# Storing the token tiles in reverse order and streaming them from last to first

## The chip, the cores and the metric

The kernel runs on one core of a Trainium2 chip. The metric is the device time of one execution in microseconds, the median of several runs. Before the change that is 657.98 us (three runs, 657.59 to 659.76).

## The reference

The inputs are q, k and v of shape (8, 8, 576, 64) in float32, two weight matrices of a first feed-forward layer (512 x 2048 and 2048 x 512), and those of a "soft" mixture of experts. Cut to what matters here:

```
x   = attention(q, k, v)                 # 4608 tokens x 512, linear attention
h   = x @ moe_w_in                       # 4608 x 2048
x2  = (h * cos(h)) @ moe_w_out           # 4608 x 512
out = soft_moe(x2, phi, w1, w2)          # logits over 32 slots, softmax both ways
```

Tokens are rows. No result depends on the order in which a product visits its tokens, as long as each result lands in the place of its token.

## The kernel before, in words

The 4608 tokens are taken in nine blocks of 512. For each block b the attention leaves x transposed in PSUM, 128 features on the partitions and tokens along the free axis. It is then split into two tiles in SBUF: XH holds x rounded to the type fp32r in which the product is formed, XL the rest x - XH. ScalarE makes XH (`x_hi`, lines 592 to 598), VectorE makes XL from PSUM and XH (`x_lo`, lines 600 to 608). In blocks 0 and 1 one instruction covers one group of 128 features and all 512 tokens (lines 598 and 608); from block 2 on one instruction covers 128 tokens of all four feature groups, through `x_views` (lines 595 and 603). That is 36 instructions on either engine, all of 128x512 elements.

Two pairs of tiles alternate, as the index `b % 2` in lines 573 to 578 says: blocks 0, 2, 4 and 6 use the pair XH0/XL0, blocks 1, 3, 5 and 7 the pair XH1/XL1. Block 8 is cut into two halves of 256 tokens, each in one tile named xe that holds both parts.

The first layer's product is `mm1` (lines 911 to 927). A block has 16 steps, one for each 128 columns of moe_w_in, and a step has 12 matmuls: four groups of features, and for each of them three products, (W high, XH), (W high, XL) and (W low, XH). The weights W are the stationary operand, a fresh 128x128 load ahead of each matmul; the token tile is streamed, 512 columns (256 in block 8):

```
for n, (wi, xi) in enumerate(((0, 0), (0, 1), (1, 0))):
    nc.tensor.matmul(
        out=u_t[s], lhsT=w[:, wi, kk, o:o + 128], rhs=x[xi][:, kk],
```

That makes 8 x 16 x 12 = 1536 matmuls of 512 columns and 2 x 16 x 12 = 384 of 256 columns, all at line 925. Each step's product lies in one of three PSUM buffers (ps_h). ScalarE or VectorE rounds it (line 933 or 935), VectorE takes the fraction (941), ScalarE the sine (946), VectorE multiplies (949), TensorE adds the step to the logits (963) and VectorE transposes the result in blocks of 32 (970).

The order of all instructions on every engine is fixed by a table of numbers, PLACES, by which the operations are sorted when the program is built. The change does not touch it: every engine issues the same instructions in the same order before and after. `mm1` of a block's first step waits for the four `x_lo` of its block; three ring buffers of ps_h tie the product to the work of the other engines three steps back.

Of the kernel before, what the change touches and what calls it, by code (L numbers as in the profile page):

```python
# [10 lines left out]
F32 = mybir.dt.float32  # L11
# [5 lines left out]
ALU = mybir.AluOpType  # L17
# [262 lines left out]
def attention_cosine_moe_softmoe(  # L280
# [21 lines left out]
    nc = tc.nc  # L302
# [16 lines left out]
    def pst(tag, bufs):  # L319
        return ps.tile([128, 512], F32, tag=tag, name="ps_" + tag, bufs=bufs)  # L320
# [140 lines left out]
    pm_t = {}  # L461
# [107 lines left out]
    def x_parts(b, t):  # L569

        i = b % 2
        if b < NB - 1:
            if xh[i] is None:
                xh[i] = sbt([128, 4, 512], "XH1", F32R)
                xl[i] = sbt([128, 4, 512], "XL1", F32R)
            return [(xh[i][:, t], xl[i][:, t], slice(0, 512))]
        if not xe:
            xe.extend(sbt([128, 2, 4, 256], tag, F32R, name="xe") for tag in ("XH0", "XL0"))
        return [(e[:, 0, t], e[:, 1, t], slice(256 * n, 256 * n + 256)) for n, e in enumerate(xe)]

    def x_views(b, e):


        x_parts(b, 0)
        px = pm_t["x", e].rearrange("p (t n) -> p t n", t=4)
        if b < NB - 1:
            o = slice(128 * e, 128 * e + 128)
            return px, xh[b % 2][:, :, o], xl[b % 2][:, :, o]
        o = slice(128 * (e % 2), 128 * (e % 2) + 128)
        return px, xe[e // 2][:, 0, :, o], xe[e // 2][:, 1, :, o]  # L590

    def x_hi(b, t):
        if b > 1:
            px, hi, lo = x_views(b, t)
            nc.scalar.copy(out=hi, in_=px)
            return
        for hi, lo, o in x_parts(b, t):
            nc.scalar.copy(out=hi, in_=pm_t["x", t][:, o])

    def x_lo(b, t):  # L600
        if b > 1:
            px, hi, lo = x_views(b, t)
            nc.vector.tensor_tensor(out=lo, in0=px, in1=hi.bitcast(F32), op=ALU.subtract)
            pm_t.pop(("x", t))
            return
        px = pm_t.pop(("x", t))
        for hi, lo, o in x_parts(b, t):
            nc.vector.tensor_tensor(out=lo, in0=px[:, o], in1=hi.bitcast(F32), op=ALU.subtract)

    def k_max(b, tp, part):  # L610

# [277 lines left out]
    u_t, t_t, lt_t = {}, {}, {}  # L889
# [4 lines left out]
    def tile_of(d, i):  # L894

        return (i + (12 if 0 < d < 8 and d % 2 == 0 else 8 if d == 8 else 0)) % NF
# [14 lines left out]
    def mm1(s, ks):  # L911
        d, f = divmod(s, NF)
        b, t0, nt = parts[d]
        f = tile_of(d, f)
        if ks[0] == 0:
            u_t[s] = pst("h", 3)[:, 0:nt]
        w = w_t[f // 2]
        o = 128 * (f % 2)
        x = (
            (xh[b % 2], xl[b % 2]) if nt == 512  # L920
            else [xe[t0 // 256][:, i] for i in range(2)]
        )
        for kk in ks:
            for n, (wi, xi) in enumerate(((0, 0), (0, 1), (1, 0))):
                nc.tensor.matmul(  # L925
                    out=u_t[s], lhsT=w[:, wi, kk, o:o + 128], rhs=x[xi][:, kk],
                    start=(kk == 0 and n == 0), stop=(kk == 3 and n == 2),
                )

# [582 lines left out]
    def q_ops(b):  # L1512
# [18 lines left out]
        if b > 1:  # L1531
            for t in range(4):
                op(("q_mul", b, t), None, 0, q_mul, b, t, after=[("q_rec", b)],
                   ways=[(POOL, 1.0, True, ()), (DVE, 0.6, True, ())])
                op(("q_blk", b, t), DVE, 0.63, q_blk, t, after=[("q_mul", b, t)])
            for bb in range(max(b - 1, 1), min(b, 7) + 1):
                if ("kv_in", bb) not in isu.ops:
                    op(("kv_in", bb), DMA, 2.0, kv_in, bb, more=1.9, data=True,
                       after=[("kv_out", bb), ("q_kv", max(bb - 1, 1), 1)])
            op(("q_kv", b, 1), PE, 1.95, q_kv4, b, take="m", n_take=4,  # L1540
               after=[*each("q_blk", b), past("kv_in", b), past("kv_in", b - 1),
                      past("mm1", 16 * b - 17)])
            for t in range(4):
                op(("x_hi", b, t), ACT, 0.48 if b < 8 else 0.6, x_hi, b, t,
                   after=[("q_kv", b, 1)])
                op(("x_lo", b, t), DVE, 0.6 if b < 8 else 0.67, x_lo, b, t,
                   give="m", after=[("x_hi", b, t)])
            return
        for tp in range(2):
            for t in (2 * tp, 2 * tp + 1):  # L1550
                op(("q_mul", b, t), None, 0, q_mul, b, t,
                   ways=[(POOL, 1.0, True, ()), (DVE, 0.6, True, ())],
                   after=[("q_rec", b)] + [past("q_tr", b if tp else b - 1, 1 - tp, h) for h in (0, 1)])
            for h in range(2):
                op(("q_tr", b, tp, h), PE, 0.48, q_tr, tp, h, take="m",
                   after=[("q_mul", b, 2 * tp), ("q_mul", b, 2 * tp + 1), past("q_kv", b - 1, tp)])
                op(("q_tr_ev", b, tp, h), None, 0, q_tr_ev, tp, h, give="m",
                   ways=[(ACT, 0.48, False, ()), (DVE, 0.6, False, ())],
                   after=[("q_tr", b, tp, h), past("q_kv", b if tp else b - 1, 1 - tp)]
                   + ([past("k_bc", b), past("k_bc", b + 1)] if b < 2 else []))  # L1560
            op(("q_kv", b, tp), PE, cost, q_kv, b, tp, take="m", n_take=2,
               after=[("q_tr_ev", b, tp, 0), ("q_tr_ev", b, tp, 1), past("k_fin", b),
                      past("k_fin", b - 1), past("mm1", 16 * b - 17)] + raw_x)
            for t in (2 * tp, 2 * tp + 1):
                op(("x_hi", b, t), ACT, 0.48 if b < 8 else 0.6, x_hi, b, t,
                   after=[("q_kv", b, tp)])
                op(("x_lo", b, t), DVE, 0.6 if b < 8 else 0.67, x_lo, b, t,
                   give="m", after=[("x_hi", b, t)])
# [43 lines left out]
    def step_ops(s):  # L1612
# [13 lines left out]
        for ks in ((0,), (1,), (2,), (3,)) if s == 0 else (range(4),):  # L1626
            op(("mm1", s) if ks[-1] == 3 else ("mm1", s, ks[-1]), PE,
               (0.7 if nt == 512 else 0.355) * len(ks),
               mm1, s, ks, take=None if ks[0] else "h",
               after=[("x_lo", b, kk) for kk in ks] * (f == 0) + [past("cD", w)] * (b == 0)  # L1630
               + [("mm1", s, ks[0] - 1) if ks[0] else past("mm1", s - 1)]
               + [past("g", s - 3)] * (ks[0] == 0))
# [246 lines left out]
```

## Time and profile before

| what | value |
|---|---|
| median of three runs | 657.98 us (657.59 to 659.76) |
| the profiled execution | 659.31 us |
| its span, first to last instruction | 657.4 us |
| TensorE busy | 625.2 us, 95% of the span |
| VectorE busy | 534.9 us, 81% |
| ScalarE busy | 365.6 us, 56% |
| GpSimd busy | 128.2 us, 20% |
| granted TensorE clock, mean | 0.986 of full speed |
| share of the last-ending chain on TensorE | 80%, of it line 925 54% |

The profiled execution is 1.33 us longer than the median; 1.9 us of its time lie outside its span. In the profile PE is TensorE's matmuls, PEld its weight loads, DVE is VectorE, ACT ScalarE, POOL GpSimd. A matmul's row shows its start and a modelled duration that runs over the start of the next one, so that the pace of a stream of matmuls is read from the distance of their starts.

### The profile page before, as it was taken

What the parts mean: (1) busy time and instruction counts of PE and PEld (TensorE: products, weight loads), DVE (VectorE), ACT (ScalarE), POOL (GpSimd) and SP (SyncE); (2) the same over time, 40 slices, a digit from 0 to 9 for tenths busy, and PEclk for the clock granted to TensorE, in tenths of its full rate; (3) what the DMA queues carried; (4) which work ended last, traced back from release to release, by engine and by line L of the source; (5) the groups of instructions that cost most, each with busy time, mean ns of one, the idle gap of its engine ahead of it and who ended that gap; (6) DMA issues with size and microseconds to landing.
All of it is one profiled execution on the core that took longest, in us unless ns stands there. A gap on an engine that the chain in (4) does not pass through costs nothing.

```text
span 657.4 us, 18204 instructions
## 1 busy us (share of the span) xinstructions
PE 625.2 (95%) x7745; PEld 472.3 (72%) x7745; DVE 534.9 (81%) x1075; ACT 365.6 (56%) x642; POOL 128.2 (20%) x131
## 2 busy tenths in 40 slices
PE   5999999999999999999999999999999999999990
PEld 4677777687868777877788788778878889853540
DVE  7889999989998988979979887878988888852251
ACT  4899988576465376446456452443645465530051
POOL 4435546052132043040230101001110000000000
PEclk9799999999999999999999999999999999999996
DMA  9998955264312242143212400013001518899968
GB/s 320 304 408 291 351 163 148 98 154 128 91 49 76 80 114 82 49 113 99 67 31 67 138 0 2 1 37 94 1 1 48 211 35 332 328 386 412 421 242 347
DMA packets 60992, 103.88 MB, mean 158 GB/s; under 512 B 9456, under 2 KB 40560, under 8 KB 55920
## 3 DMA queue, kind: packets, MB, share of 16 engines
q1 hardware_dynamic: 60912, 102.74, 45.9%
q8 instruction: 60, 0.98, 0.6%
q14 instruction: 20, 0.16, 0.1%
HBM read 88.15 MB, written 14.57 MB: 156 GB/s over the span
## 4 chain that ended last, share of the span: by engine, by line
PE 80%; DMA 7%; DVE 6%; ACT 2%; issue 1%; POOL 1%; SPq 0%; DVEq 0%; ACTq 0%
PE ps_h L925 54%; PE ps_m L1110 6%; PE ps_LT L963 4%; PE ps_m L713 2%; PE ps_m L528 2%; PE ps_m L1357 2%; DMA rwo<-in_moe_w_out_dram 2%; DMA Q<-in_q_dram 2%; PE ps_LT L1699 2%; DMA KVB<-in_k_dram 1%; DMA out_dram<-ob 1%; DMA G<-in_moe_w_out_dram 1%; PE ps_h L1315 1%; PE ps_m L1315 1%; DVE qm L422 1%
## 5 line engine op out<-in xcount | busy, mean ns | idle before, releaser
L925 PE MATMUL ps_h<-XH,W 128*128 128x512 f32 x1024 | 330.1, 397 | 2.2 <-DVE G L949 2.2
L925 PEld LDWEIGHTS ps_h<-XH,W 128*128 128x128 f32 x1024 | 192.3, 188 | 56.8 <-issue 7.1
L925 PE MATMUL ps_h<-XL,W 128*128 128x512 f32 x512 | 201.0, 393 | 0.0
L946 ACT ACTIVATE T<-T 128x512 f32<-128x512 f32 (+1 forms) x160 | 92.7, 587 | 90.8 <-DVE T L941 90.4
L933 ACT ACTIVATE T<-ps_h,quarter 128x512 int32<-128x512 f32 (+1 forms) x123 | 79.3, 646 | 87.0 <-PE ps_h L925 86.6
L949 DVE TENSOR_TENSOR G<-T,ps_h 128x512 f32<-128x512 f32 (+1 forms) x160 | 99.2, 623 | 21.0 <-ACT T L946 15.7
L925 PEld LDWEIGHTS ps_h<-XL,W 128*128 128x128 f32 x512 | 96.2, 188 | 20.0
L941 DVE SCALAR_TENSOR_TENSOR T<-T,ps_h 128x512 f32<-128x512 int32 (+1 forms) x160 | 98.9, 622 | 10.6 <-ACT T L933 9.4
L970 DVE STREAM_TRANSPOSE G<-G 128x512 f32<-128x512 f32 (+1 forms) x160 | 98.2, 637 | 0.3 <-PE ps_LT L963 0.2
L425 POOL TENSOR_TENSOR Q<-Q,qm 128x512 f32<-128x512 f32 x33 | 34.8, 1072 | 153.7 <-DVE qm L422 128.2
L689 POOL TENSOR_TENSOR KVB<-KVB,km 128x576 f32<-128x576 f32 x22 | 33.3, 1539 | 72.3 <-DVE km L682 51.3
L925 PE MATMUL ps_h<-xe,W 128*128 128x256 f32 x384 | 46.7, 281 | 0.0
L925 PEld LDWEIGHTS ps_h<-xe,W 128*128 128x128 f32 x384 | 45.3, 189 | 1.6 <-DVE G L949 0.8
L446 POOL TENSOR_TENSOR Q<-Q,qm 128x512 f32<-128x512 f32 x27 | 27.9, 1061 | 82.6 <-DVE qm L439 63.3
L963 PE MATMUL ps_LT<-G,wphi 128*32 128x128 f32 (+1 forms) x1280 | 38.7, 264 | 0.8 <-issue 0.8
L963 PEld LDWEIGHTS ps_LT<-G,wphi 128*32 128x32 f32 x1280 | 30.4, 109 | 8.9 <-issue 6.7
L1110 PE MATMUL ps_m<-G,A 32*32 32x512 f32 x1024 | 35.7, 597 | 0.0
L946 ACT ACT_TABLE_LOAD x24 | 30.8, 1283 | 0.4
L935 DVE TENSOR_SCALAR T<-ps_h 128x512 int32<-128x512 f32 (+1 forms) x37 | 22.7, 614 | 7.1 <-PE ps_h L925 6.9
L422 DVE TENSOR_REDUCE qm<-Q 128x8 f32<-128x512 f32 x36 | 24.0, 672 | 3.2 <-DMA Q<-in_q_dram 3.2
L1110 PEld LDWEIGHTS ps_m<-G,A 32*32 32x32 f32 x1024 | 16.9, 103 | 13.4 <-issue 8.1
L1128 DVE SCALAR_TENSOR_TENSOR gacc<-gacc,ac,ps_m 128x512 f32<-128x512 f32 x32 | 23.2, 732 | 2.3 <-PE ps_m L1110 2.3
(214 smaller groups left out, 715.6 us busy)
## 6 DMA issues: line engine op xcount, KB each, us to landing
w_u<-in_moe_w_dram SPq DMA_DIRECT2D x22, 1024.0 KB, 8.1
KVB<-in_k_dram SPq DMA_DIRECT2D x16, 576.0 KB, 5.1
KVB<-in_v_dram SPq DMA_DIRECT2D x32, 256.0 KB, 4.4
out_dram<-ob SPq DMA_DIRECT2D x8, 1024.0 KB, 8.9
rwi<-in_moe_w_in_dram SPq DMA_DIRECT2D x7, 1024.0 KB, 9.9
G<-in_moe_w_dram SPq DMA_DIRECT2D x7, 1024.0 KB, 7.0
rwo<-in_moe_w_out_dram SPq DMA_DIRECT2D x5, 1024.0 KB, 10.5
wo<-G SPq DMA_DIRECT2D x16, 256.0 KB, 4.5
```

The lines of the kernel that those rows point to most:

```text
L422: nc.vector.reduce_max(out=qm[:, t], in_=qv(t), axis=AX.X)
L425: (nc.vector if eng == "DVE" else nc.gpsimd).tensor_tensor(out=qv(t), in0=qv(t), in1=qm[:, t].unsqueeze(2).to_broadcast([128, 8, 64]), op= ...
L446: (nc.vector if eng == "DVE" else nc.gpsimd).tensor_tensor(out=qv(t), in0=qv(t), in1=qs[:, t].unsqueeze(2).to_broadcast([128, 8, 64]), op= ...
L689: (nc.vector if eng == "DVE" else nc.gpsimd).tensor_tensor(out=k_t[:, t], in0=k_t[:, t], in1=km[:, t].unsqueeze(1).to_broadcast([128, KC, ...
L925: nc.tensor.matmul(out=u_t[s], lhsT=w[:, wi, kk, o:o + 128], rhs=x[xi][:, kk], start=(kk == 0 and n == 0), stop=(kk == 3 and n == 2),)
L933: nc.scalar.activation(out=t.bitcast(I32), in_=u_t[s], func=ACTF.Identity, bias=quarter)
L941: nc.vector.scalar_tensor_tensor(out=t, in0=t.bitcast(I32), scalar=0.25, in1=u_t[s], op0=ALU.subtract, op1=ALU.subtract)
L946: nc.scalar.activation(out=t_t[s], in_=t_t[s], func=ACTF.Sin, scale=-UNDER_TWO_PI)
L949: nc.vector.tensor_tensor(out=g_of(s), in0=t_t.pop(s), in1=u_t.pop(s), op=ALU.mult)
L963: nc.tensor.matmul(out=lt_t[d][32 * c:32 * c + 32, 0:w], lhsT=w2sb[:, f], rhs=g[:, w * c:w * c + w], start=(f0 == 0), stop=(f0 == NF - 1),)
L970: nc.vector.transpose(out=g_of(s), in_=g_of(s))
L1110: nc.tensor.matmul(out=st["gp"][i][32 * c:32 * c + 32].rearrange("p (f b) -> p f b", f=NF) if d < NB else st["gp"][i][32 * c:32 * c + 32]. ...
```

## The change

The tokens of a block are stored in XH and XL in reverse order: token n of the block in column 511 - n (in block 8, column 255 - n of its half). For this the copies read PSUM backwards, and from block 2 on write their 128 tokens into the mirrored slice of columns. The products then stream the columns backwards, with a step of -1, so that the results in PSUM stand in the natural order again.

```diff
--- before.py
+++ after.py
@@ -582,11 +582,11 @@
         x_parts(b, 0)
-        px = pm_t["x", e].rearrange("p (t n) -> p t n", t=4)
+        px = pm_t["x", e].rearrange("p (t n) -> p t n", t=4)[:, :, ::-1]
         if b < NB - 1:
-            o = slice(128 * e, 128 * e + 128)
+            o = slice(384 - 128 * e, 512 - 128 * e)
             return px, xh[b % 2][:, :, o], xl[b % 2][:, :, o]
-        o = slice(128 * (e % 2), 128 * (e % 2) + 128)
+        o = slice(128 - 128 * (e % 2), 256 - 128 * (e % 2))
         return px, xe[e // 2][:, 0, :, o], xe[e // 2][:, 1, :, o]
@@ -595,7 +595,7 @@
         for hi, lo, o in x_parts(b, t):
-            nc.scalar.copy(out=hi, in_=pm_t["x", t][:, o])
+            nc.scalar.copy(out=hi, in_=pm_t["x", t][:, o][:, ::-1])
@@ -605,7 +605,7 @@
         for hi, lo, o in x_parts(b, t):
-            nc.vector.tensor_tensor(out=lo, in0=px[:, o], in1=hi.bitcast(F32), op=ALU.subtract)
+            nc.vector.tensor_tensor(out=lo, in0=px[:, o][:, ::-1], in1=hi.bitcast(F32), op=ALU.subtract)
@@ -923,7 +923,7 @@
                 nc.tensor.matmul(
-                    out=u_t[s], lhsT=w[:, wi, kk, o:o + 128], rhs=x[xi][:, kk],
+                    out=u_t[s], lhsT=w[:, wi, kk, o:o + 128], rhs=x[xi][:, kk, ::-1],
                     start=(kk == 0 and n == 0), stop=(kk == 3 and n == 2),
                 )
```

## Rows read from the trace of the kernel before

**Rows 1.** The page: busy time and share, then the granted clock in 40 slices.
```profile
PE 625.2 (95%) x7745; PEld 472.3 (72%) x7745; DVE 534.9 (81%) x1075; ACT 365.6 (56%) x642; POOL 128.2 (20%) x131
...
PEclk9799999999999999999999999999999999999996
```

**Rows 2.** The page: the chain that ended last, by engine and by line.
```profile
PE 80%; DMA 7%; DVE 6%; ACT 2%; issue 1%; POOL 1%; SPq 0%; DVEq 0%; ACTq 0%
PE ps_h L925 54%; PE ps_m L1110 6%; PE ps_LT L963 4%; PE ps_m L713 2%; PE ps_m L528 2%; PE ps_m L1357 2%; DMA rwo<-in_moe_w_out_dram 2%; DMA Q<-in_q_dram 2%; PE ps_LT L1699 2%; DMA KVB<-in_k_dram 1%; DMA out_dram<-ob 1%; DMA G<-in_moe_w_out_dram 1%; PE ps_h L1315 1%; PE ps_m L1315 1%; DVE qm L422 1%
```

**Rows 3.** Groups by line and shape, TensorE: busy us, mean ns, idle before.
```profile
L925 PE MATMUL ps_h<-XH,W 128*128 128x512 f32 x1024 | 330.1, 397 | 2.2 <-DVE G L949 2.2
L925 PE MATMUL ps_h<-XL,W 128*128 128x512 f32 x512 | 201.0, 393 | 0.0
L925 PE MATMUL ps_h<-xe,W 128*128 128x256 f32 x384 | 46.7, 281 | 0.0
```

**Rows 4.** Timeline of TensorE in block 4 (pair XH0/XL0): start us, us.
```profile
328.70 0.39 PE L925 MATMUL ps_h<-XL,W 128*128 128x512 f32 x1
328.93 0.63 PE L925 MATMUL ps_h<-XH,W 128*128 128x512 f32 x2
329.40 0.40 PE L925 MATMUL ps_h<-XL,W 128*128 128x512 f32 x1
...
344.80 0.40 PE L925 MATMUL ps_h<-XL,W 128*128 128x512 f32 x1
```

**Rows 5.** The same in block 3 (pair XH1/XL1).
```profile
267.09 0.39 PE L925 MATMUL ps_h<-XL,W 128*128 128x512 f32 x1
...
282.73 0.39 PE L925 MATMUL ps_h<-XL,W 128*128 128x512 f32 x1
```

**Rows 6.** The same in block 8 (xe tiles).
```profile
539.66 12.99 PE L925 MATMUL ps_h<-xe,W 128*128 128x256 f32 x108
```

**Rows 7.** Timeline of the weight loads in block 4.
```profile
328.47 0.19 PEld L925 LDWEIGHTS ps_h<-XL,W 128*128 128x128 f32 x1
328.71 0.42 PEld L925 LDWEIGHTS ps_h<-XH,W 128*128 128x128 f32 x2
329.17 0.19 PEld L925 LDWEIGHTS ps_h<-XL,W 128*128 128x128 f32 x1
```

**Rows 8.** Busy time by stretch: us, PE, PEld, DVE, ACT, POOL, PEclk, DMA, GB/s.
```profile
104.00:164.00 60.00, 60.00 (x846) 46.94 (x845) 55.92 (x115) 40.20 (x66) 22.12 (x19) 1.00 0.44 124
...
328.24:345.04 16.80, 16.80 (x74) 13.54 (x72) 12.04 (x22) 9.74 (x15) 5.76 (x4) 1.00 0.16 36
266.64:282.96 16.32, 16.32 (x74) 13.51 (x72) 15.21 (x31) 7.24 (x12) 4.45 (x4) 1.00 0.18 50
```

**Rows 9.** Groups by line and shape, VectorE and ScalarE: the copies into XH and XL.
```profile
L603 DVE TENSOR_TENSOR XL<-ps_m,XH 128x512 fp32r<-128x512 f32 x24 | 15.9, 675 | 0.2
L608 DVE TENSOR_TENSOR XL<-ps_m,XH 128x512 fp32r<-128x512 f32 x8 | 5.5, 694 | 1.1 <-ACT XH L598 1.0
...
L595 ACT CAST XH<-ps_m 128x512 fp32r<-128x512 f32 x24 | 13.2, 587 | 6.2 <-PE ps_m L528 6.2
L598 ACT CAST XH<-ps_m 128x512 fp32r<-128x512 f32 x8 | 4.6, 594 | 1.1 <-PE ps_m L565 1.1
```

**Rows 10.** The same view: two VectorE reads of PSUM, line 1294 every fourth element.
```profile
L1294 DVE TENSOR_SCALAR KVB_u<-ps_m,esacc 128x512 f32<-128x512 f32 x1 | 0.8, 751 | 2.6 <-PE ps_m L1285 2.6
L1329 DVE TENSOR_SCALAR hs<-ps_h,mask 128x512 f32<-128x512 f32 x1 | 0.8, 751 | 8.5 <-PE ps_h L1315 8.5
```

**Rows 11.** The chain that ended last, in order of time: start us, us.
```profile
28.27 0.59 ACT XH L598
...
238.11 1.88 DVE XL L603 x3
```

## The prediction

> **What bounds the kernel now.** I read the page first, then the chain that ended last, then the groups by line, and last the timeline of single matmuls. The page shows TensorE busy for 95% of the span, with the clock at its full level in all but the first and the last slices [rows 1]. The chain says that this is no accident of averaging: 80% of it is TensorE, and 54% of the span is line 925, the streamed product of the first layer [rows 2]. The groups show that these matmuls almost never wait: 2.2 us of idle time in front of 1024 of them and none in front of the other 896 [rows 3]. So from about 30 to 575 us the end is set by the pace at which line 925 streams columns, and that is the operand that the change turns round.
>
> The durations in the groups overlap, so the pace has to be read from starts. In block 4 the (W high, XL) matmul, one in three, starts at 328.70 and 23 periods later at 344.80: 16.10 us for 69 matmuls, 233.3 ns each [rows 4]. In block 3 it is 15.64 us for 69, 226.7 ns each [rows 5]. In block 8 the last of 108 half-length matmuls starts 12.99 - 0.28 = 12.71 us after the first [rows 3, 6]: 118.8 ns for 256 columns. All three lie above the pure column time at the granted 2.4 GHz, 213.3 and 106.7 ns (the granted share was 1.00 in the first two stretches [rows 8]): by 20.0 ns, by 13.3 ns, and by 12.1 ns.
>
> This excess is the interesting part. Blocks 3 and 4 use the same weights, the same PSUM buffers and the same instructions; what differs is the pair of token tiles. The engine waits for nothing in either. So something small is lost while the columns are read, and how much depends on where the read tile lies. Each weight load starts with a matmul, takes 0.19 us and so runs beside the streaming [rows 7]: it is the nearest candidate for what the stream meets, but the trace doesn't prove it.
>
> **The change, part by part.**
>
> *The ScalarE copies (x_hi), 36 of them.* They read PSUM backwards instead of forwards and write as many elements: 587 and 594 ns each, some 20 us in all with the four of block 8, which are of the same shape [rows 9]. ScalarE is busy for 56% of the span [rows 1].
>
> *The VectorE subtractions (x_lo), 36 of them.* 675 and 694 ns each, some 24 us in all [rows 9]. Does reading PSUM in another order cost VectorE anything? The nearest row is line 1294, which reads PSUM at every fourth element and takes 751 ns; line 1329, the same operation read in order, takes 751 ns too [rows 10]. I take 0 for both engines. The upper bound is a doubling. Most of it would lie under TensorE's stream, because a block's copies run while the steps of the block before are still being streamed; on the chain these copies appear for only 0.59 us and 1.88 us [rows 11], so a doubling puts some 2.5 us on the path. If that cover went, VectorE would be late first: it was busy for 55.92 of 60 us in the stretch from 104 to 164 [rows 8]. Below nothing I see no way: the row that reads out of order is no faster either.
>
> *The mirrored slices.* From block 2 on, each copy writes the mirrored 128 columns. A matmul reads all four slices and waits for all four copies, before and after, so it makes no difference which slice comes first: 0.
>
> *The matmuls, 1536 of 512 columns and 384 of 256.* Same number, same order, same weight loads; the moving operand has a step of -1. No row of this trace has such an operand. The bounds: below, the whole excess goes, 768 x 20.0 + 768 x 13.3 + 384 x 12.1 ns = 15.4 + 10.2 + 4.6 = 30.2 us less (each pair of tiles has four of the eight full blocks). Above, a backward read could run at one column in the time of two: 1536 x 213.3 + 384 x 106.7 ns = 369 us more. Between ends so far apart I take the value nearest to the rows that are nearest: every column is still read once, neighbours still follow neighbours, and both pairs of tiles stay where they are, so the pace of each pair stays, 0.
>
> The Trainium skill, page "TensorE: Matmul & The Clock Gate", section "Step-by-step: what each phase is for", says that TensorE reads the moving operand and the weights through two ports of their own, so that the next weights take no read bandwidth from the running matmul. By that rule nothing between the two reads could depend on a direction and the sum would be 0; by the rows, with two paces for two pairs of tiles, it may be anything from -30 to a similar gain in the other direction. The same skill, page "SBUF — State Buffer", section "Specifications (TRN2)", gives SBUF 16-byte lines of which at least two hits are needed for full bandwidth; a step of -1 has four hits per line like a step of 1, so this page speaks against a halved rate. No run here shows either.
>
> **The sum.** 0 + 0 + 0. The sum is made on the profiled execution (span 657.4 us, 659.31 us in all), which is 1.33 us above the median of the runs; as the sum is a difference of 0, I forecast the median, 658.0 us. A measurement of this kernel can tell about 0.3% from no change, 2.0 us. In the pace that is little: 1536 + 384/2 = 1728 matmuls of full length, so 1.15 ns of 230 decide.
>
> **The rivals.**
>
> *Fewer meetings in the stream (faster).* If the excess comes from two reads that meet, turning one of them round changes how often. For it: the excess exists, it depends on the tile, and it is not waited for. Against it: nothing says which direction is the better one. Prices: if the blocks of XH0/XL0 only reached the pace of XH1/XL1, 768 x 6.7 ns = 5.1 us less, 653; if the whole excess went, 30.2 us less, 628. VectorE would give some of that back, as it has only 4 us free in 60 in the early blocks [rows 8]. I put the middle at half the excess, 15 us: 643 us.
>
> *More meetings in the stream (slower).* The same mechanism with the other sign, in the same place: each matmul of line 925 takes longer, TensorE stays the bound and everything behind it moves. From a mean pace of (233.3 + 226.7) / 2 + 1.15 = 231.2 ns on it decides. Prices: all at the pace of XH0/XL0, 768 x 6.7 ns = 5.1 us more, 663; the excess doubled, 30.2 us more, 688. Nothing on the other engines would hide it, since line 925 is on the chain with its whole length [rows 2].
>
> *A backward read at half the rate (slower).* Each matmul takes its column time once more: 658 + 369 = 1027 us. Three matmuls would then take over 1.3 us in place of 0.70. For it only that no row shows the form; it is a cliff, so there is no middle.
>
> That the change doesn't do what it says would show as forward reads and unchanged rows; the instructions of every engine are the same in number and order, so it can't be told from the first case by time.
>
> **How the numbers follow.** Unchanged pace 0.35 (656 to 660 us by itself), fewer meetings 0.30, more meetings 0.22, half the rate 0.13. The likeliest is the unchanged pace, 658.0 us. Within 0.3%: 0.33, leaving 0.02 of the first case for copies that come a little late. Faster: 0.30. Slower: 0.02 + 0.22 + 0.13 = 0.37. The half rate is left out of the range, and the outer ends of the two neighbours with it, 0.07 together: from 634 us, 24 of the 30 us of excess gone, to 688 us, the excess doubled.
>
> **What would show it.** Right: in blocks 3 and 4 three matmuls of line 925 take 0.680 and 0.700 us as before, the idle time in front of them stays at about 2 us, and lines 595, 598, 603 and 608 keep their mean durations within 20 ns. Fewer or more meetings: that period moves, in both pairs or in one, while weight loads keep their 0.19 us. Half rate: the modelled duration of a full matmul jumps by some 200 ns. The copies are wrong if lines 595 or 603 take over 1 us and line 925's idle time grows. The whole argument is wrong if the period stays and the end moves, because then the pace of line 925 wasn't what set it.

## The result and the profile after

| | before | after |
|---|---|---|
| median of nine runs on the same chips | 659.76 us (657.59 to 663.08) | 665.34 us (662.72 to 667.79) |
| ratio after / before | | 1.0081, 95% interval 1.0055 to 1.0107 |
| the profiled execution, its span | 659.31 us, 657.4 us | 662.72 us, 660.8 us |

The kernel became slower by 0.8%: 0.0081 x 659.76 = 5.3 us, by the interval 3.6 to 7.1 us. The page of the changed kernel, busy times, granted clock and the two lines of the chain:

```profile
PE 628.6 (95%) x7745; PEld 471.6 (71%) x7745; DVE 534.7 (81%) x1075; ACT 366.0 (55%) x642; POOL 128.3 (19%) x131
...
PEclk8999999999999999999999999999999999999996
...
PE 77%; DMA 8%; DVE 5%; ACT 4%; SPq 2%; issue 1%; DVEq 0%; ACTq 0%
PE ps_h L925 55%; PE ps_m L1110 6%; PE ps_LT L963 4%; DMA w_u<-in_moe_w_dram 3%; PE ps_m L528 2%; PE ps_m L713 2%; DMA KVB<-in_k_dram 2%; DMA out_dram<-ob 1%; PE ps_h L1315 1%; DMA rwi<-in_moe_w_in_dram 1%; SPq L388 1%; PE ps_LT L1699 1%; DMA A<-kd 1%; DVE G L970 1%; PE ps_m L1033 1%
```

The same engine at the same clock, the same number of instructions, and line 925 still has more than half of the chain (55%, 54% in [rows 2]). TensorE alone is busy longer, by 3.4 us; VectorE, ScalarE and GpSimd stand within 0.5 us of [rows 1]. The groups by line and shape of the changed kernel say where (busy us, mean ns, idle before):

```profile
L925 PE MATMUL ps_h<-XH,W 128*128 128x512 f32 x1024 | 333.8, 401 | 3.1 <-DVE G L949 3.1
L925 PE MATMUL ps_h<-XL,W 128*128 128x512 f32 x512 | 203.4, 397 | 0.0
...
L925 PEld LDWEIGHTS ps_h<-XL,W 128*128 128x128 f32 x512 | 96.3, 188 | 21.4 <-DVE XL L608 0.2
L925 PE MATMUL ps_h<-xe,W 128*128 128x256 f32 x384 | 47.2, 283 | 0.0
...
L603 DVE TENSOR_TENSOR XL<-ps_m,XH 128x512 fp32r<-128x512 f32 x24 | 15.9, 674 | 0.2
L595 ACT CAST XH<-ps_m 128x512 fp32r<-128x512 f32 x24 | 13.2, 586 | 6.3 <-PE ps_m L528 6.3
...
L608 DVE TENSOR_TENSOR XL<-ps_m,XH 128x512 fp32r<-128x512 f32 x8 | 5.4, 686 | 0.4 <-ACT XH L598 0.4
L598 ACT CAST XH<-ps_m 128x512 fp32r<-128x512 f32 x8 | 4.7, 601 | 1.1 <-PE ps_m L565 1.1
```

The three groups of line 925 are busy for 3.7, 2.4 and 0.5 us more than in [rows 3] (they overlap, so these are not to be added), and the idle time in front of them grew by only 0.9 us. The copies stand within 8 ns of [rows 9]: here reading PSUM backwards cost neither engine anything. The weight loads keep the 188 ns that they had before:

```profile
L925 PEld LDWEIGHTS ps_h<-XL,W 128*128 128x128 f32 x512 | 96.2, 188 | 20.0
```

So it is the pace, and the timeline of TensorE shows which pace. Block 3, the pair XH1/XL1, the same 69 matmuls as in [rows 5] (start us, us):

```profile
267.04 0.40 PE L925 MATMUL ps_h<-XL,W 128*128 128x512 f32 x1
...
283.14 0.40 PE L925 MATMUL ps_h<-XL,W 128*128 128x512 f32 x1
...
328.43 0.40 PE L925 MATMUL ps_h<-XL,W 128*128 128x512 f32 x1
...
344.53 0.40 PE L925 MATMUL ps_h<-XL,W 128*128 128x512 f32 x1
```

The second pair of lines is block 4, the pair XH0/XL0, as in [rows 4]. Both stretches now take 16.10 us, 233.3 ns a matmul. Block 4 took that before too; block 3 took 15.64 us, 226.7 ns. The difference between the two pairs of tiles is gone, and it went on the slow side.

Over whole blocks, as the mean distance of neighbouring starts inside the steps (the few wider than 290 ns left out), blocks 0, 2, 4 and 6 have 233.3 ns in both kernels, and blocks 1, 3, 5 and 7 go from 227.9 to 233.4 ns. That is 768 x 5.5 ns = 4.2 us. Block 8 takes 59.33 us from the start of its first to that of its last matmul in place of 58.76, 0.6 us more. The sum, 4.8 us, lies inside the measured 3.6 to 7.1.

The two profiled executions lie 3.4 us apart. The stretch from the first to the last start of a full matmul shows the same thing in them (the kernel before, then the changed one; us, PE busy, and so on as in [rows 8]):

```profile
31.24:516.46 485.22, 478.90 (x5688) 374.08 (x5685) 430.64 (x820) 295.73 (x492) 115.76 (x110) 1.00 0.34 105
30.13:518.41 488.28, 482.82 (x5689) 374.21 (x5685) 430.32 (x820) 296.44 (x492) 114.88 (x110) 1.00 0.34 105
```

TensorE is busy for 3.9 us more in it; 0.9 us of that is taken back by shorter waits.

### The profile page after: what moved, and what is told of

Read it like the earlier page. It is cut to its first block, busy times and chain, and to the rows that moved or that the text cites. A ratio compares the mean times of both kernels' runs of the same rounds, so it can differ in the third digit from the quotient of the medians.

```text
span 660.8 us, 18204 instructions
## 1 busy us (share of the span) xinstructions
PE 628.6 (95%) x7745; PEld 471.6 (71%) x7745; DVE 534.7 (81%) x1075; ACT 366.0 (55%) x642; POOL 128.3 (19%) x131
## 4 chain that ended last, share of the span: by engine, by line
PE 77%; DMA 8%; DVE 5%; ACT 4%; SPq 2%; issue 1%; DVEq 0%; ACTq 0%
PE ps_h L925 55%; PE ps_m L1110 6%; PE ps_LT L963 4%; DMA w_u<-in_moe_w_dram 3%; PE ps_m L528 2%; PE ps_m L713 2%; DMA KVB<-in_k_dram 2%; DMA out_dram<-ob 1%; PE ps_h L1315 1%; DMA rwi<-in_moe_w_in_dram 1%; SPq L388 1%; PE ps_LT L1699 1%; DMA A<-kd 1%; DVE G L970 1%; PE ps_m L1033 1%
## 5 line engine op out<-in xcount | busy, mean ns | idle before, releaser
L925 PE MATMUL ps_h<-XH,W 128*128 128x512 f32 x1024 | 333.8, 401 | 3.1 <-DVE G L949 3.1
L925 PE MATMUL ps_h<-XL,W 128*128 128x512 f32 x512 | 203.4, 397 | 0.0
```

The lines of the kernel that those rows point to most:

```text
L925: nc.tensor.matmul(out=u_t[s], lhsT=w[:, wi, kk, o:o + 128], rhs=x[xi][:, kk, ::-1], start=(kk == 0 and n == 0), stop=(kk == 3 and n == 2),)
```

## The experiments

A single run is no fine measure here: nine runs of the kernel before lie between 657.59 and 663.08 us. So the verdicts rest on the pace in the traces, which repeats from run to run to a few tenths of a nanosecond where nothing was changed (odd blocks forwards: 227.7 to 227.9), and on the time only where a run was repeated (e10). The kernel before, timed beside each group of experiments, took 658.0 to 660.1 us. "Stretch" in the table is the same 69 matmuls in every kernel, read as above; "mean" is over the starts inside the steps of four whole blocks, without the few that follow at more than 290 ns.

| kernel | time us | block 3 stretch | block 4 stretch | mean odd blocks | mean even blocks |
|---|---|---|---|---|---|
| before | 659.76 (9 runs) | 226.7 | 233.3 | 227.9 | 233.3 |
| after | 665.34 (9 runs) | 233.3 | 233.3 | 233.4 | 233.3 |
| e1 odd blocks backwards | 663.66 | 233.3 | 233.3 | 233.4 | 233.4 |
| e2 even blocks backwards | 662.49 | 226.7 | 233.3 | 227.9 | 233.3 |
| e3 forwards, 64 bytes of pad | 666.56 | 226.7 | 233.3 | 227.8 | 232.8 |
| e4 forwards, 960 bytes of pad | 658.78 | 226.7 | 226.7 | 227.8 | 227.9 |
| e5 forwards, staggered weights | 663.57 | 231.8 | 232.0 | 231.0 | 231.2 |
| e6 backwards, staggered weights | 664.83 | 233.3 | 233.3 | 233.4 | 233.6 |
| e9 backwards, 960 bytes of pad | 667.21 | 233.3 | 233.3 | 233.4 | 233.4 |
| e10 forwards, pads modulo 256 | 656.43 (12 runs) | 226.7 | 226.7 | 227.7 | 227.8 |
| e11 forwards, 32 columns of weights | 659.64 | 231.3 | 231.7 | 231.1 | 231.4 |
| e12 backwards, 32 columns of weights | 664.62 | 233.3 | 233.3 | 233.4 | 233.5 |
| e13 groups of 16 from last to first | 663.31 | 233.3 | 235.6 | 233.3 | 234.8 |
| e14 16 columns of a group from last to first | 714.08 | 266.7 | 266.7 | 266.7 | 266.7 |

### Which blocks pay: e1 and e2

Both kernels are the changed one with the turn left on for some blocks only; the others, block 8 among them, store and stream as before.

```diff
+    def back(b):
+        return b % 2 == 1                  # e2: b % 2 == 0 and b < NB - 1
+    def turn(b, ap):
+        return ap[:, ::-1] if back(b) else ap
...
-                    ... rhs=x[xi][:, kk],
+                    ... rhs=turn(b, x[xi][:, kk]),
```

> Only blocks 1, 3, 5 and 7 (pair XH1/XL1) are stored and streamed backwards; blocks 0, 2, 4, 6 and 8 are as before. Theory 1 (the change costs only where the forward stream stood well against the weights, in XH1/XL1): those four blocks go from about 228 to 233 ns a matmul, the others stay at 233, and the time is some 4 to 5 us above before, nearly all of the change's cost. Theory 2 (reading backwards costs a little in every block and other waits make up the sum): about half of the cost, 2 to 3 us, and no block at 233 that was at 227.

> Only blocks 0, 2, 4 and 6 (pair XH0/XL0) are stored and streamed backwards. Theory 1: those blocks stay at 233 ns, the odd ones stay at about 228, block 8 as before, and the time is that of before within 1 us. Theory 2: 2 to 3 us more than before, the pace of the even blocks above 233.3.

Odd blocks backwards lift exactly the odd blocks, to 233.4 ns; even blocks backwards change no pace at all. On the timeline, block 3 of e1 (backwards), then block 3 (forwards) and block 4 (backwards) of e2:

```profile
268.08 0.40 PE L933 MATMUL ps_h<-XL,W 128*128 128x512 f32 x1
...
284.18 0.40 PE L933 MATMUL ps_h<-XL,W 128*128 128x512 f32 x1
...
268.64 0.39 PE L933 MATMUL ps_h<-XL,W 128*128 128x512 f32 x1
...
284.28 0.39 PE L933 MATMUL ps_h<-XL,W 128*128 128x512 f32 x1
...
329.78 0.40 PE L933 MATMUL ps_h<-XL,W 128*128 128x512 f32 x1
...
345.88 0.40 PE L933 MATMUL ps_h<-XL,W 128*128 128x512 f32 x1
```

So the 4.2 us come from the pair XH1/XL1 alone. The time of e2 is some 3 us above what its paces say. It is one run, and lies inside the spread of the kernel before; no more is read from it.

### What makes the forward pace good: e3, e4

In the built program the tiles XH1 and XL1 and the eight weight tiles start at the same address modulo 1024 bytes, while XH0 and XL0 start 64 bytes lower. From here on "distance" is the start of the streamed tile less that of the weight tile, modulo 1024 bytes: 0 for the one pair and 960 for the other. PADS gives the unused bytes ahead of a tile. A larger one ahead of wphi, which lies behind XL0, moves the weights and the pair XH1/XL1 together, by 64 bytes in e3 and 960 in e4:

```diff
-    PADS = {'wphi': 32}
+    PADS = {'wphi': 96}                    # e4: 992
```

> The kernel before, all forwards, with 64 bytes more of unused space between the tiles XH0/XL0 and everything allocated behind them, the weights and XH1/XL1 among that. XH0/XL0 so get another distance to the weights, XH1/XL1 keep theirs but move by 64 bytes. Theory A (the distance between the streamed tile and the weights decides, counted in steps of 128 bytes): the even blocks go from 233.3 to 226.7 ns, the odd ones stay, and the time falls by some 4 to 5 us. Theory B (the streamed tile's own place decides): the even blocks stay at 233.3 and the odd ones change. Theory C (neither, the pair's names only stand for the neighbours of the block in time): no change in either.

> As the run with 64 bytes, with 960 bytes of space: XH0/XL0 then stand at the same distance from the weights as XH1/XL1, counted in steps of 1024 bytes. Theory A: even blocks at 226.7 ns, odd ones unchanged, 4 to 5 us less than before; if here but not with 64 bytes, the pattern repeats over more than 128 bytes. Theory B: even blocks at 233.3, odd ones changed. Theory C: no change.

960 bytes bring XH0 and XL0 to distance 0 as well, and the even blocks fall to 227.9 ns. The timeline of e4 in block 4:

```profile
326.64 0.39 PE L925 MATMUL ps_h<-XL,W 128*128 128x512 f32 x1
...
342.28 0.39 PE L925 MATMUL ps_h<-XL,W 128*128 128x512 f32 x1
```

15.64 us for the 69 matmuls that took 16.10 in [rows 4]. XH1 and the weights moved by the same 960 bytes and the odd blocks kept their pace. It is the distance that counts, not the tile's own place. At distance 896 (e3) the even blocks stay slow, 232.8 ns, so the guess that the pattern repeats every 128 bytes missed. Block 8 does not share the gain: its tiles lie in the buffers of XH0 and XL0, and at distance 0 it takes 60.09 us in place of 58.76.

The two times say less than the paces. By its paces and block 8, e4 should gain 2.9 us; it came out 0.7 us below the one run beside it. e3 should have stayed level and took 666.56 us, more than any of the nine runs of the kernel before. Part of that is seen in its trace: after a wait of 1.77 us for VectorE in block 4, TensorE's granted clock was 0.50, the 1.2 GHz level, for some 3 us, and the seven starts in it lie 427 ns apart (they are left out of the mean):

```profile
301.50:304.50 3.00, 3.00 (x8) 2.30 (x7) 2.90 (x6) 1.43 (x3) 0.00 (x0) 0.50 0.00 0
```

From the start of the last matmul of block 8 to the end e3 took 86.1 us, the kernel before 81.9. No run shows that either comes from the pad.

### All distances, both directions: e5 and e6

Here a 64-byte pad stands ahead of each of the eight weight tiles, so that each lies at another distance from the streamed tiles; e6 adds the same pads to the changed kernel.

```diff
-    PADS = {'wphi': 32}
+    PADS = {'wphi': 32, 'W7': 64, 'W0': 64, 'W6': 64, 'W1': 64, 'W5': 64, 'W4': 64, 'W2': 64, 'W3': 64}
```

> The kernel before, all forwards, with 64 bytes of unused space ahead of each of the eight weight tiles, so that each stands 64 bytes further from the token tiles than its neighbour: distances (token tile minus weights, modulo 1024 bytes) of 448, 512, ... 960. Only the weights' places differ from step to step of one block. Theory A (the weight load that runs beside the stream is what it meets): the pace steps with the weight tile within one block, between 226.7 and some 240 ns, and at one distance the two pairs agree. If the pattern repeats after 512 bytes, the distance 512 gives 226.7 like the distance 0 of the run with 960 bytes, and 448 gives 233 like 960. Theory B (only the token tile's own place counts): one pace per block, 233.3 in the even and 227 in the odd ones.

> The same eight distances with the changed kernel, all backwards. Theory A, first form (a backward stream has a good distance of its own): at one or two of the eight distances the pace is 227 or below, at the others 230 to 240. [...]

Mean pace by distance, in ns, each value from 83 to 88 starts of four blocks. A distance that both pairs of tiles meet has two values, XH0/XL0 first; semicolons separate the distances:

| distance | its remainder by 256 | forwards (e5) | backwards (e6) |
|---|---|---|---|
| 512; 768 | 0 | 228.2, 228.1; 229.7, 229.6 | 233.4, 233.3; 233.6, 233.4 |
| 576; 832 | 64 | 229.2, 229.6; 229.5, 229.2 | 233.4, 233.5; 233.4, 233.3 |
| 640; 896 | 128 | 232.8, 233.0; 232.8, 232.3 | 235.0, 233.3; 233.4, 234.1 |
| 448; 704; 960 | 192 | 233.5; 233.3, 233.2; 233.2 | 233.3; 233.4, 233.3; 233.3 |

Forwards, the distance modulo 256 decides: best at 0, worst at 128 and 192. The two steps of a weight tile read columns that lie 512 bytes apart, so each value is a mean over two distances, 512 bytes apart; taken singly the two differ by at most 1.3 ns. Backwards it is 233.3 to 233.6 at 14 of 16 places, 234.1 and 235.0 at the other two, and nowhere better: a good distance of its own, as the expectation for e6 had it, did not show at any of the eight. How abruptly it changes forwards is seen on the timeline of e5 where one step ends and the next takes the next weight tile, with the streamed tile unchanged:

```profile
294.64 0.39 PE L925 MATMUL ps_h<-XL,W 128*128 128x512 f32 x1
...
296.68 0.39 PE L925 MATMUL ps_h<-XL,W 128*128 128x512 f32 x1
297.38 0.40 PE L925 MATMUL ps_h<-XL,W 128*128 128x512 f32 x1
...
299.47 0.39 PE L925 MATMUL ps_h<-XL,W 128*128 128x512 f32 x1
```

With W6 (distance 768) nine matmuls take 2.04 us, 226.7 ns each; with W7 (distance 896) 2.09 us, 232.2 ns. In e6 the same two stretches take 2.10 us each, 233.3 ns:

```profile
295.07 0.40 PE L925 MATMUL ps_h<-XL,W 128*128 128x512 f32 x1
...
297.17 0.40 PE L925 MATMUL ps_h<-XL,W 128*128 128x512 f32 x1
297.87 0.40 PE L925 MATMUL ps_h<-XL,W 128*128 128x512 f32 x1
...
299.97 0.40 PE L925 MATMUL ps_h<-XL,W 128*128 128x512 f32 x1
```

### The good distance, used backwards and forwards: e9 and e10

e9 is the changed kernel with the pad of e4. e10 is the kernel before with pads that bring XH0 and XL0 to distances 512 and 768 and hold the tiles of block 8, which share their buffers, 64 bytes lower:

```diff
-    PADS = {'wphi': 32}
+    PADS = {'XL0': 192, 'wphi': 224}
...
-    xh = [sbt([128, 4, 512], "XH0", F32R), None]
-    xl = [sbt([128, 4, 512], "XL0", F32R), None]
+    x0 = [sbt([128, 2064], t, F32R)[:, 16:2064].rearrange("p (a n) -> p a n", a=4)
+          for t in ("XH0", "XL0")]
+    xh, xl = [x0[0], None], [x0[1], None]
...
-            xe.extend(sbt([128, 2, 4, 256], tag, F32R, name="xe") for tag in ("XH0", "XL0"))
+            xe.extend(sbt([128, 2064], tag, F32R, name="xe")[:, 0:2048]
+                      .rearrange("p (i a n) -> p i a n", i=2, a=4) for tag in ("XH0", "XL0"))
```

> The changed kernel with the 960 more bytes of padding that put both pairs of XH and XL at distance 0 (mod 1024) from the weights, where the forward stream runs at 226.7 ns in all blocks. Theory 1 (backwards there is one pace, whatever the distance): 233.3 to 233.5 ns in all eight blocks, 664 to 667 us. Rival (the distance matters backwards too, and 0 is only a bad one with XH1/XL1): the even blocks differ from the odd ones by over 1 ns.

> The kernel before with pads only, forward streams: XH0 and XL0 lie at distances 512 and 768 (mod 1024) from the weights, multiples of 256, at which the kernel with staggered pads held the locked pace of 226.7 ns in part of its steps; the split tiles xe lie 64 bytes lower, at 448 and 704, so as not to pay the 121.9 ns that distance 0 cost them. If the distance modulo 256 decides: even blocks at 227 to 229 ns as the odd ones, block 8 at 117 to 119, 768 x 5 ns = 3.8 us less than before, a ratio of 0.994. If only distance 0 modulo 1024 will do: even blocks stay at 230 to 233 and the time within 1 us of before. If XH and XL at different distances disturb each other: even blocks above 233 and a slower kernel.

Backwards the pad that helped e4 does nothing: 233.4 ns in all blocks, and 16.10 us in block 4 of e9:

```profile
331.48 0.40 PE L925 MATMUL ps_h<-XL,W 128*128 128x512 f32 x1
...
347.58 0.40 PE L925 MATMUL ps_h<-XL,W 128*128 128x512 f32 x1
```

Forwards a remainder of 0 by 256 is enough: the even blocks run at 227.8 ns, and block 8 takes 58.51 us. On the timeline of e10, block 4 takes the 15.64 us that only block 3 took before:

```profile
326.55 0.39 PE L927 MATMUL ps_h<-XL,W 128*128 128x512 f32 x1
...
342.19 0.39 PE L927 MATMUL ps_h<-XL,W 128*128 128x512 f32 x1
```

The time: 656.43 us over 12 runs against 660.09 over 17 of the kernel before, ratio 0.9951, interval 0.9932 to 0.9970, so 2.0 to 4.5 us less. The paces promise 768 x 5.5 + 768 x 0.2 ns + 0.25 us = 4.6 us, a little more than arrives. This version beats both kernels.

### Is it the weights that the stream meets: e11 and e12

Ten of a step's twelve products get a quarter of their weight columns, in the kernel before (e11) and in the changed one (e12). The kernels so leave out these ten products for three quarters of the hidden units; the streams stay:

```diff
+                m = 128 if (kk, n) in ((0, 0), (3, 2)) else 32
                 nc.tensor.matmul(
-                    out=u_t[s], lhsT=w[:, wi, kk, o:o + 128], ...
+                    out=u_t[s][0:m], lhsT=w[:, wi, kk, o:o + m], ...
```

> The kernel before (streams first to last), but the 10 inner ones of a step's 12 first-layer matmuls load 32 columns of weights instead of 128, so that they leave out three quarters of the hidden units; the streams and their number stay. Theory 1 (the nanoseconds above the column time come from the stream's reads meeting the reads of the next weights): with a quarter of the weight reads the excess of 20.0 ns (XH0/XL0) and 13 to 15 ns (XH1/XL1) falls to about a quarter, 3 to 6 ns, so 217 to 219 ns between inner matmuls in every block, and the kernel gains at most 12 ns x 10/12 x 1536 = 15 us, 643 us, if nothing else takes over the end. Rival 2 (a fixed price of each matmul, whatever its weights): paces stay at 233.3 and 227 to 229 and the time at 660.

> The changed kernel with the same cut of the inner weights to 32 columns. Theory 1 (meetings with the weight reads): the backward stream loses its 20 ns as the forward one does, 217 to 219 ns between inner matmuls, and the two kernels with 32 columns come out within 2 us of each other. Rival 3 (the backward stream itself is slower, whatever the weights do): the backward pace stays near 233.3 while the forward one falls, and the two kernels lie up to 15 x 10/12 x 1536 ns = 19 us apart. Rival 2 (a fixed price per matmul): both stay.

The groups of e11 show that the ten loads did shrink, from 188 to 109 ns (108 in e12):

```profile
L926 PEld LDWEIGHTS ps_h<-XL,W 128*32 128x32 f32 x512 | 55.6, 109 | 50.8
L926 PEld LDWEIGHTS ps_h<-XH,W 128*128 128x128 f32 x256 | 48.1, 188 | 35.5 <-issue 6.9 <-PE ps_h L926 3.0 <-DVE G L950 2.8
```

No expectation came true in full. Theory 1 wanted 217 to 219 ns: neither kernel comes near it. Forwards the paces move, but towards each other: the even blocks fall from 233.3 to 231.4 ns, the odd ones rise from 227.9 to 231.1. Backwards nothing moves, as rival 3 said (its other half, a forward pace that falls, came in the even blocks alone), and the timeline of e12 in block 3 could be that of the changed kernel:

```profile
268.24 0.40 PE L926 MATMUL ps_h<-XL,W 128*32 128x512 f32 x1
...
284.34 0.40 PE L926 MATMUL ps_h<-XL,W 128*32 128x512 f32 x1
```

So the excess above the column time is not paid per weight column that is read beside the stream. The weights set the forward pace through where they lie and how wide they are; the backward pace moved with neither, but for the two places of e6.

### Is it the step of -1: e13 and e14

Tiles stored as before; the stream is cut into groups of 16 columns (64 bytes), and either the groups or the columns inside them are taken from last to first. The rest of the kernel is left as it was, so these products meet the tokens in another order than it takes them to have.

```diff
-                    ... rhs=x[xi][:, kk],
+                    ... rhs=x[xi][:, kk].rearrange("p (l n) -> p l n", n=16)[:, ::-1],
+                    # e14: [:, :, ::-1]
```

> The kernel before, tiles stored as before, but each first-layer product streams its 512 columns (256 in the last block) in groups of 16, the groups from last to first and the 16 columns of a group from first to last. The storage is not turned to match, so the products meet the tokens in another order than the rest of the program takes them to have. Theory 1 (what fixes the pace at 233.3 ns is that the stream walks down through the memory, group by group): all blocks at 233.3 to 233.5 as in the changed kernel, 663 to 667 us. Rival (it is the step of -1 between neighbouring columns): the paces of before stay, 233.3 in even blocks and 227 to 229 in odd ones, 658 to 661 us. Rival (any pattern with breaks in it costs): a third value, the same in this run and in the one with groups in order.

> The counterpart: groups of 16 columns from first to last, the 16 columns of a group from last to first, storage as before, so again the products meet the tokens in another order than the rest of the program takes them to have. Theory 1 (walking down group by group): the paces of before, 233.3 in even blocks and 227 to 229 in odd ones, 658 to 661 us. Rival (the step of -1 between neighbouring columns): 233.3 to 233.5 in all blocks, 663 to 667 us. Rival (breaks in the pattern cost): the same third value as with the groups turned.

e13 has no step of -1 between neighbours of a group, and still pays what the change pays: 233.3 ns in odd blocks. In the even ones it is a little worse, 234.8. The timeline of e13 in block 3:

```profile
268.04 0.40 PE L925 MATMUL ps_h<-XL,W 128*128 128x512 f32 x1
...
284.14 0.40 PE L925 MATMUL ps_h<-XL,W 128*128 128x512 f32 x1
```

Walking down through the tile in groups is enough, and as e13 stores its tiles as before, the turned storage is not needed for the loss. What the 31 jumps between groups add by themselves is not shown; no run has jumps and walks up with its columns in order. e14, whose groups go up, was expected at the paces of before by theory 1 and at 233.3 ns by its rival, and both missed. The timeline of e14 in block 3:

```profile
286.50 0.43 PE L925 MATMUL ps_h<-XL,W 128*128 128x512 f32 x1
...
304.90 0.43 PE L925 MATMUL ps_h<-XL,W 128*128 128x512 f32 x1
```

18.40 us for 69, 266.7 ns each, in every block: 53.3 ns above the column time of 213.3. The sum over blocks is 768 x 38.8 + 768 x 33.4 ns + 6.5 us in block 8 = 61.9 us; the run lost 54.3. Most of the rest was taken in by waits that went away. From the first to the last start of a full matmul TensorE now waits for 0.2 us (532.57 - 532.35), in the kernel before for 6.3 (485.22 - 478.90):

```profile
30.79:563.36 532.57, 532.35 (x5688) 379.90 (x5685) 433.67 (x820) 299.37 (x492) 115.07 (x110) 1.00 0.31 96
```

The rival that breaks in the pattern cost one same price falls too, since the two kernels have as many breaks and differ by some 32 ns and more. Why turning the columns inside a group costs more than turning everything stays open.

## Why the prediction was right and wrong, point by point

**The bound.** Right. Line 925 sets the end: its pace moved, and the time followed by about the sum of the paces, in the change and, with the other sign, in e10.

**The copies and the mirrored slices, 0.** Right: 674 and 686 ns, 586 and 601 ns. On the chain in order of time they stand for 0.69 + 1.07 + 0.60 + 1.87 = 4.2 us, in [rows 11] for 2.5:

```profile
27.79 0.69 DVE XL L608
...
30.24 1.07 ACT XH L598 x2
...
103.06 0.60 DVE XL L608
...
237.75 1.87 DVE XL L603 x3
```

The chain takes another way there, but no group of copies became longer by more than 7 ns, and TensorE's waits between the first and the last full matmul fell, from 6.3 to 5.5 us.

**The matmuls, 0.** This is the step that failed. It took "the pace of each pair stays", because every column is still read once and both pairs stay where they are. Blocks 0, 2, 4 and 6 did keep their 233.3 ns. Blocks 1, 3, 5 and 7 did not: 227.9 to 233.4. The step read the two paces as a property of the two tiles. They were a property of the tile's distance to the weights, and of a stream that runs upwards; the turned stream had no good distance among those tried, as e6 and e9 show. Two of the paces under the bounds were also those of single stretches: over whole blocks the odd ones had 227.9 ns and not 226.7, and block 8 116.1 ns, or 118.2 with its few wide starts, and not 118.8. The lower bound of some 30 us less hardly changes by that.

**More meetings in the stream.** This is the case that came. Its cheap price, all blocks at the pace of XH0/XL0 for 5.1 us, is what happened within its working: the blocks do stand there, and the measured 5.3 us lie 0.2 us from it. That they lie so close is in part luck: the terms by the traces are 4.2 us (the odd blocks had 227.9 before) and 0.6 us in block 8, which the price left out. The doubled excess, 688, did not come. That 665.34 us lies between 634 and 688 speaks little for the forecast, as that stretch is ten times as wide as the change; this case had a chance of 0.22, the one held to be likeliest, with 0.35, did not come. The picture behind the case, of two reads that meet, is only half borne out. Forwards the place of the weights decides the pace (e5), so the stream does feel the weights beside it. But e12 took three quarters of the weight columns from ten loads in twelve, and the backward pace did not move.

**Fewer meetings.** It did not come, and in e6 no distance tried brought it. The 5.1 us that it priced for the blocks of XH0/XL0 are there to be had, but forwards: e10 got 2.0 to 4.5 of them.

**Half the rate.** It fell: a step of -1 took 233.3 ns, and not 426.7. The trace agrees there with the Trainium skill, page "SBUF — State Buffer", section "Specifications (TRN2)", by which two hits on a 16-byte line are enough for full bandwidth. That rule alone does not explain e14, whose columns fall on each line as often and took 266.7 ns.

**The two reads.** With one streamed tile and two weight tiles e5 measured 226.7 and 232.2 ns. The trace differs there from the Trainium skill, page "TensorE: Matmul & The Clock Gate", section "Step-by-step: what each phase is for": if the next weights took nothing from the running matmul, the pace could not depend on where they lie. The measurement decides; 0, the sum by that rule, was not what came.

**Left open.** Why a stream that runs down has 233.3 ns at nearly every distance tried. Whether its direction matters by itself or only against the order in which the weights are read, no run shows. How stream and weights disturb each other at all, and why a distance modulo 256 bytes counts, no run shows either. The distances tried are multiples of 64 bytes.

## What to carry to other kernels

Where matmuls follow each other without a wait and still stand some nanoseconds above their column time, read the pace from the starts, tile by tile: two paces under the same instructions point to addresses, not to work. With fp32r operands and 128-column weights here, a forward stream whose distance to the weights is a multiple of 256 bytes ran at 227.7 to 229.7 ns per 512 columns, elsewhere at up to 233.5, so a pad of a few hundred bytes is worth trying before any edit of the program's order; here it gave 0.5% (e10). A stream that ran down had nothing to gain from a pad. Judge such an edit by the pace in the trace, as single times of this kernel spread over 5 us.

## What was not expected of the hardware

- The pace of these matmuls depends on the distance between the streamed tile and the weights that are loaded beside it, modulo 256 bytes: 228.1 to 229.7 ns at 0, 229.2 to 229.6 at 64, 232.3 to 233.0 at 128, 233.2 to 233.5 at 192 (e5).
- For 256 columns the order of distances is another one: at distance 0, good for 512 columns, block 8 took 60.09 us (e4), at 448 and 704 it took 58.51 (e10).
- A stream that runs down through its tile has 233.3 to 233.6 ns at nearly every distance tried (e6, e9; 234.1 and 235.0 at two places of e6) and also with a quarter of the weight columns in ten loads of twelve (e12), and it needs no step of -1 to be as slow (e13).
- With 16 columns taken backwards inside groups that run forwards, 512 columns take 266.7 ns (e14), 33 ns more than with the whole stream turned.
